# Two more pairs turned by DMA, turns ahead of far loads in the sync queue, and two waits of loads for weight transfers

## The chip, the cores and the metric

The kernel runs on one core of a Trainium2 chip. The core has five engines that run at once, each with its own instruction queue, taken in order: TensorE (PE) for matrix products, VectorE (DVE), ScalarE (ACT) and GpSimd (POOL) for element-wise work, and SyncE (SP), which here only issues transfers. Sixteen DMA engines carry what SP and POOL issue. The metric is the device time in microseconds, the median of three runs.

## The reference

`q`, `k` and `v` have the shape (4, 8, 768, 64): batch, heads, positions, width. The first half is attention over blocks of 64 keys; each query keeps its own block and the three with the highest gate score. The second half is a Fourier mixing, a normalisation and an MLP.

```python
k_rep = k.reshape(B, H, n_blocks, block, D).mean(axis=3)
gate_scores = np.einsum('bhsd,bhnd->bhsn', q, k_rep)
...
top_idx = np.argsort(gate_scores, axis=-1)[..., -top_k:]
...
scores = scale * np.matmul(q, k.transpose(0, 1, 3, 2))
mask = mask & (pos[:, None] >= pos[None, :])
...
return np.matmul(attn, v).astype(np.float32)
```
```python
X = np.fft.fft(x, axis=1)
X = np.fft.fft(X, axis=2)
u = x + np.real(X).astype(np.float32)
...
un = (u - mu) / np.sqrt(var + 1e-06)
ch = np.maximum(un @ w_ch1, 0.0) @ w_ch2
return (u + ch).astype(np.float32)
```

`x` is the attention output of one batch, 768 × 512; `w_ch1` is 512 × 2048 and `w_ch2` 2048 × 512. Inputs and output are float32.

## The kernel before

**Pairs.** `attention(p)` treats two heads at a time, 16 pairs in all, four to a batch. For a pair it loads `k`, `q` and `v` of both heads (six transfers, `load`, issued at line 476 on SP's queue), casts them to float16 (`_copy`, lines 833 and 834) and forms the residuals of `q` and `k` (lines 589 and 594, on POOL for most pairs). `k` and `q` must then be turned, so that the width lies on partitions. Up to pair 6 this is done on PE: `k_turn` (line 606) makes six 128 × 128 transposes for both heads together, `q_turn` (line 672) six for each head, into a PSUM bank, and DVE or ACT copies the bank out (two copies for `k`, two for `q`, lines 833 and 834). From pair 7 on (`TURN_K = 7` for `k`, a literal 7 for `q`) it is done by DMA transposes on SP's queue: two of `k` (line 614) and two of `q` (line 663). Then come the key sums (line 635), their spread (line 652), the gates (line 692, or 687 from pair 6 on), the choice of the top three (lines 706 to 744; from pair 6 on POOL sets the own block at line 739), the turn of the mask (line 751), its writing under the turned `q` (line 761), the scores (line 784) with the exponential on ACT (line 796) and, from pair 5 on, the causal select on POOL (line 802), and the product with `v` (line 814), which DVE normalises into `x` (lines 823 and 826).

**Batches.** `fourier(b)` follows the four pairs of a batch: sums on DVE (lines 846 to 867), products on PE (885 to 929), `u` (lines 944 to 967), statistics and the normalised rows (lines 974 to 1005), and their turn into `unT`, by SP's DMA transposes (line 1017) except for the first three row tiles of batch 0, which PE turns (line 1025). `mlp(b)` is the up-projection (line 1129), the ReLU (1141 on ACT, 1143 on DVE), the down-projection (1158), the addition (1164) and the output. The last batch's down-projection goes by seven block products (1103).

**Weights.** `w1` comes in eight transfers and `w2` in eight more, cast on the way, issued by POOL (line 480). Each has a planned release: 37.0 + 1.8 i for `w1`, `W2` + 1.8 g for `w2`, with `W2 = 55.0`.

**Order.** All operations are given to a planner, `Plan`, with a rank, the engines that may run them with a cost, and what they read and write. `schedule` lays them out on the five queues by start time and then rank. `search` repeats this with random shifts of ranks and releases, grouped by rank or by release, and keeps a shift that doesn't lengthen the plan. The program's instructions are emitted in the order of the plan found; after that each engine's queue is fixed, and on the chip an instruction waits only for its semaphores. Where the plan leaves PE idle before 75 us, `filler` (line 498) puts in products whose result nobody reads. For pair 7 (`p == HP + 3`) the loads name `("w1", 3, 1)`, the last transfer of `w1`, as read; that orders the plan but is no wait on the chip. The loads of pairs 6 and later use two of three slots in turn (`slot`), so pair 8 takes the slot of pair 6, and pair 7 that of pair 4.

Of the kernel before, what the change touches and what calls it, by code (L numbers as in the profile page):

```python
# [81 lines left out]

class Op:
    __slots__ = ("i", "rank", "engs", "fn", "deps", "users", "ps", "wait", "ready",
                 "done", "eng", "start", "dma", "port", "rel", "fill", "hold", "turn")


class Plan:
# [21 lines left out]
        return p  # L110

    def op(self, rank, engs, fn, r=(), w=(), ps=(), dma=0.0, port=False, pre=(), after=(), rel=0.0,
           turn=False):
        o = Op()
        o.turn = turn
        o.rel, o.fill, o.hold = rel, 0, None
        o.i, o.rank, o.engs, o.fn = len(self.ops), rank, engs, fn
        o.deps, o.users, o.ps, o.dma, o.port = set(), [], list(ps), dma, port
        o.eng = o.start = o.done = None
        for k in r:  # L120
            if k in self.last_w:
# [12 lines left out]
        for k in w:  # L134
            self.last_w[k] = o.i
            self.readers[k] = []
        for p in o.ps:
            if p in self.last_w and p not in r and p not in w:
                o.deps.add(self.last_w[p])
            p.left += 1  # L140
        o.deps.discard(o.i)
        self.ops.append(o)
        return o
# [12 lines left out]
    def search(self, rounds, seed):  # L156
# [1 line left out]
        rng = random.Random(seed)  # L158
        groups = {}
        for o in self.ops:  # L160
            if 0 < o.rank < 30000:
                groups.setdefault(("rank", o.rank), []).append(o)
            if o.rel > 59.0:
                groups.setdefault(("rel", o.rel), []).append(o)
# [3 lines left out]
        for _ in range(rounds):  # L168
            what = rng.random()
# [158 lines left out]

LATE = 2600
SYM = (1, 2, 3)  # L330
W2 = 55.0
TURN_K = 7


def release(p):
# [24 lines left out]
def kernel(  # L360
# [12 lines left out]
    HP = H // 2  # L373
# [7 lines left out]
    eng = dict(PE=nc.tensor, ACT=nc.scalar, DVE=nc.vector, POOL=nc.gpsimd, SP=nc.sync)  # L381
# [13 lines left out]
    w1 = sb([128, 4, DF], F16, "w1")  # L395
    w2 = sb([128, NIT, DM], F16, "w2")
# [75 lines left out]
    P = Plan()  # L472


    def dma(rank, e, dst, src, w, us, r=(), issue=0.58, rel=0.0):
        P.op(rank, {e: issue if e != "POOL" else 0.65}, lambda x, n: eng[x].dma_start(dst, src),  # L476
             r=r, w=w, dma=us, rel=rel)

    def weight(rel, dst, src, w):
        P.op(-1000, {"POOL": 0.65}, lambda x, n: nc.gpsimd.dma_start(out=dst, in_=src),  # L480
# [46 lines left out]
    def slot(p):  # L527
        return p % 3 if p < 6 else p % 2

    def load(p, rank, what, e, q_="SP", r=()):  # L530
# [30 lines left out]
    def attention(p):  # L561
# [8 lines left out]
        if p:  # L570
            at_ = 1.7 + 0.1 * p if p < 3 else base - 2900
            for e in range(2):
                load(p, at_, "k", e, r=[("w1", 3, 1)] if p == HP + 3 else ())
                load(p, at_, "q", e, r=[("w1", 3, 1)] if p == HP + 3 else ())
            for e in range(2):
                load(p, at_ + (0.1 if p < 3 else 500), "v", e,
                     r=[("w1", 3, 1)] if p == HP + 3 else ())
        for e in range(2):
            hi = qhl[h2][:, e, :, AT[e]:AT[e] + 64]
            lo = qhl[h2][:, e, 1:NST, 64 - AT[e]:128 - AT[e]]  # L580
# [29 lines left out]
                 w=[tk], ps=[tk], pre=[("ki", 0, g3), ("ki", 1, g3)])  # L610
        for e in range(2):
            if p >= TURN_K:
                P.op(base + 16, {"SP": 1.4},
                     lambda x, n, e=e: nc.sync.dma_start_transpose(
                         out=ki_all[:, g3, 3 * e:3 * e + 3].rearrange("p s e c -> p (s e) c"),
                         in_=kx[h2][:, 3 * e:3 * e + 3, :].rearrange("p s c -> p (s c)")),
                     r=[("k16", h2, 0), ("k16", h2, 1), ("kone", h2)], w=[("ki", e, g3)],
                     pre=[("ki", 1 - e, g3)], turn=True)
                continue
# [38 lines left out]
                                 .rearrange("p (e c) -> p e c", e=2)),  # L658
              r=[ks], w=[("gh", g2)], ps=[ks])
        for e in range(2):  # L660
            if p >= 7:
                P.op(base + 14 + e, {"SP": 1.4},
                     lambda x, n, e=e: nc.sync.dma_start_transpose(
                         out=QG[e][g3].rearrange("p (s c) -> p s c", s=NST),
                         in_=qhl[h2][:, e].rearrange("p s c -> p (s c)")),
# [568 lines left out]
```

## Time and profile before

| | |
|---|---|
| median of 3 runs | 292.82 us (292.0 to 293.37) |
| profiled execution, device time | 294.43 us |
| its span, first to last instruction | 292.7 us |
| PE, DVE, ACT, POOL busy | 285.5, 216.0, 185.5, 142.0 us |
| matrix products on PE | 2965 |
| read from HBM, written | 28.58 MB, 6.29 MB |
| granted TensorE clock | 1.000 |

In the lines of the profile a group shows its source line, engine and operation, its output and inputs by the program's names, and after the bar the busy time and the mean in ns. A window shows the busy time of each engine in a stretch of the span. In a timeline the first number is the start in us and the second the length; brackets give idle time before, and what ended it. `SPq` is SP's queue, where a transfer's issue is counted, and "to landing" is from issue to completion. A matmul's record contains its pipeline's fill, so the steps of the chain of waits, rather than the means of groups, tell how much PE time a run of matmuls takes.

### The profile page before, as it was taken

How to read it: one execution, taken by the hardware profiler on the slowest of the kernel's cores; microseconds unless marked ns; L12 is line 12 of the kernel's file. 1: busy time of each engine (PE TensorE's matmuls, PEld its weight loads, DVE VectorE, ACT ScalarE, POOL GpSimd, SP SyncE). 2: the span in 40 equal slices, each digit the busy share in tenths (PEclk: the TensorE clock that was granted, in tenths of full speed). 3: DMA queues.
4: the chain of work that ended last, by engine and by line, in shares of the span. 5: the costliest groups of instructions: out<-in, count | busy, mean ns of one | idle time of the engine just before them, and what ended most of it. 6: DMA issues, size and time to landing. Idle time of an engine off the chain costs nothing.

```text
span 292.7 us, 8027 instructions
## 1 busy us (share of the span) xinstructions
PE 285.5 (98%) x2965; PEld 191.9 (66%) x2965; DVE 216.0 (74%) x744; ACT 185.5 (63%) x419; POOL 142.0 (49%) x269
## 2 busy tenths in 40 slices
PE   8999999999999999999899999999999999999995
PEld 3778777776656686566556676556655754566884
DVE  5879898899634879986255869989818796057884
ACT  3469999787925587479617866939672681577000
POOL 7467987667776638787608473870220030000000
PEclk9999999999999999999999999999999999999999
DMA  8999998999889977878869549454001006300132
GB/s 209 266 236 231 232 211 133 207 236 217 133 180 212 211 179 158 198 168 192 154 112 226 147 91 188 88 136 105 3 35 45 31 0 115 102 2 0 36 111 72
DMA packets 123191, 41.04 MB, mean 140 GB/s; under 512 B 115608, under 2 KB 119352, under 8 KB 123152
## 3 DMA queue, kind: packets, MB, share of 16 engines
q1 hardware_dynamic: 118672, 35.67, 55.4%
q0 software_dynamic: 3552, 4.56, 9.3%
q8 instruction: 23, 0.38, 0.5%
q10 hardware_dynamic: 928, 0.30, 0.4%
q14 instruction: 16, 0.13, 0.2%
HBM read 28.58 MB, written 6.29 MB: 119 GB/s over the span
## 4 chain that ended last, share of the span: by engine, by line
PE 86%; DMA 5%; SPq 3%; ACT 1%; POOL 1%; issue 1%; DVE 1%; ACTq 0%
PE bank L1129 25%; PE bank L1158 21%; PE bank L784 11%; PE bank L1103 6%; PE bank L814 6%; PE bank L498 5%; DMA loads<-in_q_dram 4%; SPq L476 3%; PE bank L885 2%; PE bank L635 1%; DMA turned<-turned 1%; PE bank L672 1%; PE bank L779 1%; PE bank L692 1%; PE bank L606 1%; PE bank L751 1%
## 5 line engine op out<-in xcount | busy, mean ns | idle before, releaser
L796 ACT ACTIVATE turned<-bank 128x512 f16<-128x512 f32 x192 | 89.5, 576 | 24.0 <-PE bank L784 23.8
L1129 PE MATMUL bank<-unT,w 128*128 128x384 f16 x512 | 90.5, 326 | 0.2 <-DVE u L967 0.2
L1141 ACT ACTIVATE hT<-bank 128x384 f16<-128x384 f32 x117 | 57.4, 498 | 29.7 <-PE bank L1129 27.0
L1158 PE MATMUL bank<-w,hT 128*128 128x512 f16 x288 | 67.9, 379 | 0.0
L1129 PEld LDWEIGHTS <-w 128*128 128x128 f16 x512 | 47.7, 97 | 29.4 <-issue 0.5
L784 PE MATMUL bank<-turned,keys 128*128 128x128 f16 (+6 forms) x384 | 50.2, 259 | 0.2 <-DVE u L967 0.2
L1158 PEld LDWEIGHTS <-hT 128*128 128x128 f16 x288 | 26.7, 97 | 27.8
L802 POOL TENSOR_SCALAR_AFFINE_SELECT turned<-turned 128x512 f16<-128x512 f16 (+1 forms) x44 | 22.7, 538 | 30.6 <-ACT turned L796 15.3
L784 PEld LDWEIGHTS <-keys 128*128 128x128 f16 (+1 forms) x384 | 29.3, 97 | 12.0 <-issue 0.4
L814 PEld LDWEIGHTS <-turned 128*128 128x128 f16 x672 | 24.2, 97 | 5.3 <-ACT turned L796 1.1
L594 POOL TENSOR_TENSOR loads<-loads 128x384 f16<-128x384 f32 x25 | 23.0, 919 | 6.3 <-DVE fs L867 2.4
L814 PE MATMUL bank<-small,turned 128*128 128x65 f16 x672 | 25.6, 193 | 0.2 <-ACT turned L796 0.2
L761 DVE TENSOR_SCALAR turned<-bank 12x384 f16<-12x384 f16 x64 | 20.4, 318 | 5.7 <-PE bank L751 3.2
L589 POOL TENSOR_TENSOR turned<-loads,turned 128x320 f16<-128x320 f32 x26 | 20.8, 800 | 5.4 <-DVE turned L834 3.0
L498 PE MATMUL bank<-bsb 128*128 128x512 f16 x75 | 21.9, 422 | 1.3 <-DVE bsb L487 1.3
L1164 DVE TENSOR_TENSOR u<-bank,u 128x512 f32<-128x512 f32 x18 | 12.4, 686 | 11.8 <-PE bank L1158 11.7
L955 POOL TENSOR_TENSOR u<-u,bsb 128x255 f32<-128x255 f32 x10 | 7.3, 726 | 22.7 <-DVE u L959 18.4
L826 DVE TENSOR_TENSOR x<-bank,small 128x384 f16<-128x384 f32 x32 | 17.7, 553 | 0.7
L823 DVE RECIPROCAL small<-bank 128x6 f32<-128x6 f32 x32 | 6.1, 191 | 13.7 <-PE bank L814 13.3
L974 DVE BATCH_NORM_STATS2 small<-u 128x6 f32<-128x512 f32 x24 | 16.0, 678 | 0.1
L834 POOL CAST small<-loads 128x384 f16<-128x384 f32 x24 | 11.8, 507 | 8.4 <-DVE pm L857 3.3
L1109 DVE TENSOR_TENSOR u<-u,bank 128x256 f32<-128x256 f32 x36 | 13.1, 415 | 3.2 <-PE bank L1103 2.2
(138 smaller groups left out, 438.7 us busy)
## 6 DMA issues: line engine op xcount, KB each, us to landing
loads<-in_k_dram SPq DMA_DIRECT2D x28, 192.0 KB, 3.4
loads<-in_v_dram SPq DMA_DIRECT2D x28, 192.0 KB, 3.7
loads<-in_q_dram SPq DMA_DIRECT2D x26, 192.0 KB, 3.5
out_dram<-u SPq DMA_DIRECT2D x18, 256.0 KB, 2.4
w<-in_moe_w_ch_dram POOLq DMA_DIRECT2D x16, 256.0 KB, 6.8
out_dram<-u SPq DMA_DIRECT2D x12, 128.0 KB, 1.7
hT<-in_k_dram SPq DMA_DIRECT2D x4, 192.0 KB, 3.8
hT<-in_q_dram SPq DMA_DIRECT2D x4, 192.0 KB, 3.9
```

The source lines that it names most:

```text
L498: nc.tensor.matmul(bank32[P.SPARE], warm[:, 0:128], warm, start=True, stop=True)
L589: lambda x, n, hi=hi, lo=lo, e=e: eng[x].tensor_tensor(out=lo, in0=qn[a][:, e, 1:NST], in1=hi[:, 1:NST], op=OP.subtract),
L594: lambda x, n, kh=kh, kl=kl, e=e: eng[x].tensor_tensor(out=kl, in0=kn[a][:, :, e, :], in1=kh, op=OP.subtract),
L761: nc.vector.tensor_scalar(out=rows[:, i::2, :], in0=turned[at:at + NB, 0:3 - i, :], scalar1=-NEG, scalar2=NEG, op0=OP.mult, op1=OP.add)
L784: nc.tensor.matmul(bank32[sp.bank][:, co:co + a1 - a0], KI[e][g3][0:ROWS[e], jt, :], QG[e][g3][0:ROWS[e], a0:a1], start=not added, stop=no ...
L796: lambda x, n, sp=sp, pt=pt, at=at, wid=wid: nc.scalar.activation(out=pt[:, at:at + wid], in_=bank32[sp.bank][:, 0:wid], func=AF.Exp, scal ...
L802: lambda x, n, pt=pt, at=at, nd=nd: nc.gpsimd.affine_select(out=pt[:, at:at + 128 * nd].rearrange("p (a c) -> p a c", a=nd), in_=pt[:, at: ...
L814: nc.tensor.matmul(o[:, st, 0:65], pt[:, col:col + 128], V16[v4][:, e, jt, 0:65], start=(i == 0), stop=(i == 20))
L826: lambda x, n, rc=rc, o_=o_, h=h: nc.vector.tensor_tensor(out=xb[b % 3][:, :, 64 * h:64 * h + 64], in0=o_()[:, :, 0:64], in1=rc.to_broadca ...
L1129: nc.tensor.matmul(bank32[hp_.bank][:, 0:384], w1[:, dt, 128 * it:128 * it + 128], unT[:, dt, 384 * hf:384 * hf + 384], start=(dt == 0), s ...
L1141: nc.scalar.activation(out=o, in_=i_, func=AF.Relu)
L1158: nc.tensor.matmul(bank32[cp.bank], hT[hf][:, it, 128 * j:128 * j + 128], w2[:, it, :], start=(it == 0), stop=(it == NIT - 1))
```

## The change

`TURN_K` becomes 5 and a new `TURN_Q = 5` takes the place of the literal 7, so `k` and `q` of pairs 5 and 6 are turned by DMA as well. The ranks of all DMA turns of `q` and `k` go down by `TOP = 2000`, two pairs' worth, against other work of the same queue, loads among it. The planner's `op` takes `behind`, a list of keys whose last writers come first; these become real dependencies of the instruction. By it the loads of pair 7 wait for the transfer `("w1", 2, 1)`, the seventh of the weights, and those of pair 8 for `("w2", 6)`, the fifteenth; pair 7's former plan-only order behind `("w1", 3, 1)` goes. `W2` is 56.0 instead of 55.0. The search has 800 rounds instead of 700 and another seed, and may now also shift groups with ranks between -5000 and 0.

```diff
-           turn=False):
+           turn=False, behind=()):
         o = Op()
+        o.behind = [self.last_w[k] for k in behind]
...
+        o.deps.update(o.behind)
         o.deps.discard(o.i)
...
-            if 0 < o.rank < 30000:
+            if -5000 < o.rank < 30000:
...
-W2 = 55.0
-TURN_K = 7
+W2 = 56.0
+BEHIND = {7: [("w1", 2, 1)], 8: [("w2", 6)]}
+TOP = 2000
+TURN_Q = 5
+TURN_K = 5
...
-            [(t, i, e)], 0.72 if p < 1 else 0.88, r=r,
+            [(t, i, e)], 0.72 if p < 1 else 0.88, behind=BEHIND.get(p, ()),
...
-                load(p, at_, "k", e, r=[("w1", 3, 1)] if p == HP + 3 else ())
-                load(p, at_, "q", e, r=[("w1", 3, 1)] if p == HP + 3 else ())
+                load(p, at_, "k", e)
+                load(p, at_, "q", e)
...
-                P.op(base + 16, {"SP": 1.4},
+                P.op(base - TOP + 16, {"SP": 1.4},
...
-            if p >= 7:
-                P.op(base + 14 + e, {"SP": 1.4},
+            if p >= TURN_Q:
+                P.op(base - TOP + 14 + e, {"SP": 1.4},
...
-        for o in P.search(700, 10):
+        for o in P.search(800, 12):
             filler(o.fill)
             made[o.i] = o.fn(o.eng, o)
-            if o.hold is not None:
-                tc.add_manual_dep(made[o.i].ins, made[o.hold.i].ins.name, mybir.DependencyInfo(
-                    mybir.DependencyClass.Sync, mybir.DependencyReason.DATA), reason="port")
+            for i in ([o.hold.i] if o.hold is not None else []) + o.behind:
+                tc.add_manual_dep(made[o.i].ins, made[i].ins.name, mybir.DependencyInfo(
+                    mybir.DependencyClass.Sync, mybir.DependencyReason.DATA), reason="order")
```

More of the change, by code (lines that the diff above doesn't have):

```diff
@@ L84 @@
     __slots__ = ("i", "rank", "engs", "fn", "deps", "users", "ps", "wait", "ready",
-                 "done", "eng", "start", "dma", "port", "rel", "fill", "hold", "turn")
+                 "done", "eng", "start", "dma", "port", "rel", "fill", "hold", "turn", "behind")
 class Plan:
@@ L472, with dma @@
     P = Plan()
-    def dma(rank, e, dst, src, w, us, r=(), issue=0.58, rel=0.0):
+    def dma(rank, e, dst, src, w, us, r=(), issue=0.58, rel=0.0, behind=()):
         P.op(rank, {e: issue if e != "POOL" else 0.65}, lambda x, n: eng[x].dma_start(dst, src),
-             r=r, w=w, dma=us, rel=rel)
+             r=r, w=w, dma=us, rel=rel, behind=behind)
     def weight(rel, dst, src, w):
@@ L528, in slot, with load @@
         return p % 3 if p < 6 else p % 2
-    def load(p, rank, what, e, q_="SP", r=()):
+    def load(p, rank, what, e, q_="SP"):
         b, hp = divmod(p, HP)
@@ L572, in attention @@
             for e in range(2):
-                load(p, at_, "k", e, r=[("w1", 3, 1)] if p == HP + 3 else ())
-                load(p, at_, "q", e, r=[("w1", 3, 1)] if p == HP + 3 else ())
+                load(p, at_, "k", e)
+                load(p, at_, "q", e)
             for e in range(2):
-                load(p, at_ + (0.1 if p < 3 else 500), "v", e,
-                     r=[("w1", 3, 1)] if p == HP + 3 else ())
+                load(p, at_ + (0.1 if p < 3 else 500), "v", e)
         for e in range(2):
```

## The prediction, made before the changed kernel ran

> **What bounds the kernel now.** I read the page's first parts, then the busy time by stage, then the waits of PE after the first up-projection.
>
> ```profile
> span 292.7 us, 8027 instructions
> PE 285.5 (98%) x2965; PEld 191.9 (66%) x2965; DVE 216.0 (74%) x744; ACT 185.5 (63%) x419; POOL 142.0 (49%) x269
> ...
> PEclk9999999999999999999999999999999999999999
> ```
> ```profile
> core 0: us, PE busy (x) PEld busy (x) DVE busy (x) ACT busy (x) POOL busy (x), PEclk, DMA share, GB/s
> ...
> 53.00:67.47 14.47, 14.28 (x169) 11.02 (x169) 13.69 (x46) 11.47 (x25) 9.69 (x18) 1.00 1.19 223
> ...
> 80.00:140.00 60.00, 59.71 (x634) 38.71 (x633) 43.94 (x154) 39.53 (x94) 42.70 (x87) 1.00 0.85 184
> 140.00:150.00 10.00, 8.81 (x83) 5.31 (x80) 3.43 (x20) 4.71 (x10) 4.07 (x10) 1.00 0.79 164
> 150.00:240.00 90.00, 90.00 (x866) 57.84 (x864) 69.67 (x212) 60.09 (x141) 37.50 (x75) 1.00 0.41 91
> 240.00:289.30 49.30, 49.23 (x343) 33.37 (x341) 31.60 (x92) 18.06 (x37) 0.67 (x1) 1.00 0.23 60
> ```
> ```profile
> PE bank L687 <- DMA turned<-turned: 1.2, 1, 1.2
> ```
> ```profile
> 53.00:67.50 14.50, 4.88 (x19) 1.66 (x18) 1.00 1.19 223
> 67.50:80.00 12.50, 0.00 (x0) 0.00 (x0) 1.00 1.07 176
> ```
>
> The clock is full in every slice (PEclk). A window's columns are its length, then busy time and count by engine. From 80 us to 289.3 us PE works without a break, but for one gap of 1.2 us near 146. Before 67.5 us its 98% is padded: the last windows are of the fillers (L498) alone, 4.88 us of the 14.5 us before MLP 0. In that stretch DVE is the full engine (13.69 of 14.47 us): it does the Fourier step of batch 0, which the first up-projection needs. So the time is the start of that up-projection, plus PE's work behind it, plus the gaps in that work. Work that leaves PE before 67.5 us helps only if DVE lets the up-projection start sooner.
>
> **The transfers of the same stretch** are the second thing to see.
>
> ```profile
> 46.10 0.37 SPq L476 DMA_DIRECT2D loads<-in_k_dram  x1
> ```
> ```profile
> 64.35 11.78 DMA loads<-in_q_dram
> ```
> ```profile
> 49.25 1.10 POOL L480 DMA_DIRECT2D w<-in_moe_w_ch_dram  x2
> ...
> 67.61 1.43 POOL L480 DMA_DIRECT2D w<-in_moe_w_ch_dram  x2
> ...
> 72.94 0.51 POOL L834 CAST loads<-loads 128x384 f16<-128x384 f32 x1 [1.47 <-DMA loads<-in_k_dram]
> ...
> 76.18 0.53 POOL L834 CAST turned<-loads 128x384 f16<-128x384 f32 x1 [1.79 <-DMA loads<-in_q_dram]
> ```
> The second fence is the chain of waits, the third POOL's timeline. Counted by pair, SP issues the loads of pair 8 first (from 46.10) and those of pair 7 last; its q takes 11.78 us beside the weights, and POOL idles for it.
>
> **The change, part by part.** *Turns of pairs 5 and 6.* 36 transposes leave PE.
>
> ```profile
> 50.05 0.34 PE bank L672 x6
> ...
> 50.68 0.89 PE bank L498 x4
> ```
> Six cost 0.34 us (those of k have the same shape), so PE loses 6 × 0.34 = 2.04 us. The changed program's order has 78 fillers where 75 stood, which adds 3 × 0.22 = 0.66. All else on PE is the same: net −1.4 us. Almost all of that (−1.5, the rest moved behind) lies ahead of the first up-projection. Can DVE follow? Eight evictions go away as well; the rows for 30 to 67 us are
>
> ```profile
> L726 DVE MAX8 mx<-gsb 128x8 f32<-128x12 f32 x40 | 3.2, 155 | 0.0
> L834 DVE COPY turned<-bank 128x768 f16<-128x768 f16 x6 | 3.1, 548 | 0.0
> ...
> L967 DVE TENSOR_TENSOR u<-bank,x 128x512 f32<-128x512 f32 x4 | 2.5, 677 | 0.0
> ...
> L730 DVE TENSOR_TENSOR gmp<-gsb,mx 128x120 f16<-128x120 f32 x1 | 0.3, 271 | 0.0
> L710 DVE TENSOR_TENSOR gsb<-bank,gsb 128x120 f32<-128x120 f32 x1 | 0.3, 264 | 0.0
> ```
> Between the last x of pair 3 and the normalising pass L1005, DVE's new order lacks two q copies (1.1), pair 6's ten MAX8 (40 take 3.2: 0.8), its L710 and L730 (0.5) and a small copy (0.2), and has one L967 more (0.68): 2.6 − 0.7 = 1.9 us less. So DVE can give the 1.4 us, and I take −1.4 in full. Bounds: 0 if DVE's chain is held by something else, −1.9.
>
> *What the turns cost elsewhere.* Eight DMA transposes join SP's queue.
>
> ```profile
> L663 SPq DMA_TRANSPOSE turned<-turned x18: 1209/1238/1512, 77.5 to 201.3; - x18
> ...
> DMA to landing us min/median/max: 2.5/2.6/4.5
> ```
> ```profile
> 47.63 0.78 POOL L589 TENSOR_TENSOR turned<-loads,turned 128x320 f16<-128x320 f32 x1 [1.07 <-DVE kg L834]
> ```
> ```profile
> 59.64 0.40 PE L687 MATMUL bank<-kg,turned 128*128 128x24 f16 x10
> ...
> 67.24 0.33 PE L751 MATMUL bank<-small,gmp 128*128 128x128 f16 x3
> 67.47 1.46 PE L1129 MATMUL bank<-unT,w 128*128 128x384 f16 x8
> ```
> Each holds SP 1.24 us, 10 us in all, at a place where SP waited anyway (its loads of 46 to 67 us move behind). Late is at worst the second q turn of pair 6: its input is ready at 47.63 + 0.78 = 48.4; one k turn goes ahead (1.24), so it lands at 49.7 + 2.6 = 52.3. No turn of the trace ran beside the weights; the nearest rows are the loads that did:
>
> ```profile
> w<-in_moe_w_ch_dram POOLq DMA_DIRECT2D x3, 256.0 KB, 7.6
> loads<-in_k_dram SPq DMA_DIRECT2D x2, 192.0 KB, 8.3
> loads<-in_q_dram SPq DMA_DIRECT2D x2, 192.0 KB, 8.7
> ```
> ```profile
> loads<-in_q_dram SPq DMA_DIRECT2D x26, 192.0 KB, 3.5
> ```
> The first three were issued from 46 to 51 us. The fourth is the page's, over all q loads of SP: 3.5 us, so company costs up to 8.7 − 3.5 = 5.2 us and the turn lands at 57.5. The gates that need it stood at 59.64; what stands ahead of them in PE's new order, each instruction at its row's time, is 2.4 us more: 62.0. Covered, with 4.5 us to spare.
>
> A rule that speaks against this part: the Trainium skill (VectorE: DVE Perf Modes, The three transpose paths, and its Rules for kernel authors) would turn a 128×128 tile on TensorE, at 390 ns there against 1309 ns by DMA. By its figure six tiles take an estimated 7.9 us; by the row above they land in 2.6, so the trace does not bear that figure out. It is priced among the rivals.
>
> *The waits.* Pair 7's loads wait for the seventh weight transfer, pair 8's for the fifteenth. Behind them in SP's queue stand pair 7's turns, then the loads of pairs 8 and 9 and pair 8's turns, then the first output and batch 0's last three unT turns. The seventh transfer left as second of the two at 49.25, at 49.8; at 7.6 us it landed near 57.5. With pair 8's six loads gone from that time it should do as those of 38 to 46 us did:
>
> ```profile
> w<-in_moe_w_ch_dram POOLq DMA_DIRECT2D x5, 256.0 KB, 5.4
> ```
> That is near 55.2, so the four k and q loads leave from 55 to 58 and land, at 3.5 to 8.7 us, by 61.5 to 66.7. I take 64, the middle: few weights are in flight then, since w2 waits on POOL for the select of pair 5 and an `fs` sum. Who waits: four casts on POOL, and behind them in its new order the last weight issue (0.7) and the four memsets of pair 6's mask (1.07, below). The mask is turned at L751, 67.24 before, and by the same count 1.2 later now: 68.4.
>
> ```profile
> 65.57 1.07 POOL L739 MEMSET gmp<- 64x5 f16 x4
> ```
> 64 + 0.5 + 0.7 + 1.1 = 66.3: in time by 2 us. At the slow end, 66.7, it is 0.6 late. Pair 8's loads come up in SP's queue only after pair 7's turns, near 71, when the fifteenth transfer is down or nearly so (it left at 67.61, the first of the last two, and six loads fewer compete); they land by 77, while POOL still has pair 7's residuals and the select of pair 6 ahead of their casts. I cost this wait at nothing; where that cover is gone pair 8's sums on PE are late, one for one.
>
> *Turns ahead of far loads, W2 one later, a longer search.* These reorder, at no work.
>
> ```profile
> 137.32 4.13 SPq L1017 DMA_TRANSPOSE unT<-x  x3
> 141.51 1.17 SPq L476 DMA_DIRECT2D loads<-in_v_dram  x2
> 142.77 1.21 SPq L663 DMA_TRANSPOSE turned<-turned  x1
> ```
> The gap at 146 is the turn issued at 142.77, queued behind two far v loads and three unT turns. The new order puts attention 5 to 10 us earlier against the MLP there, so this gap (1.2 us) goes; but a new order of 225 us on a full PE may open its own. Bounds: −1.2 to +2.4 (two such gaps more than are lost); I take −0.6, half the gap.
>
> **Sum.** −1.4 − 0.6 = −2.0 us: the span 292.7 becomes 290.7. The profiled execution itself took 294.43 (1.7 around its span), and the runs shown have a median of 292.82, close to the span; so 290.8 us.
>
> **Rivals.** (1) *Hidden anyway.* The up-projection still starts at 67.5 and the freed PE time turns into fillers; what moved behind (0.1) and half the gap at 146 leave 292.82 + 0.1 − 0.6 = 292.3. For it: PE has 4.88 us of fillers there already. Against: DVE, the full engine, loses 1.9 us.
>
> (2) *More.* The start gains DVE's full 1.9, the gap at 146 goes whole and nothing opens: 292.82 − 1.9 − 1.2 = 289.7. Against: a new order rarely has no gap of its own.
>
> (3) *Pair 7's loads hold POOL: slower.* The seventh weight lands at 57.5 as before, the loads leave until 60.5 and take 8.7 to 11.78 us: 69.2 to 72.3. Cast, issue and memsets bring pair 6's mask to 71.5 to 74.6 against 68.4. PE stands in order at L751, with the up-projection behind it: 3.1 to 6.2 us, the middle 4.6. 292.82 − 1.4 + 4.6 = 296.0. It decides from the point where the fourth load lands after 66.1. For it: every load of 46 to 65 us was this slow. Against: six of them are what the wait moves away.
>
> (4) *Late turns: slower.* Beside the weights the turns could take 8.7 us, as the loads did, and one after the other: pair 6's last two then end at 48.4 + 17.4 = 65.8, 3.8 behind the gates: 292.82 − 1.4 + 3.8 = 295.2. By the skill's estimated 7.9 us each they would end at 64.2, and the time be 293.6. Against: the 18 turns of L663 landed in 2.5 to 4.5 us while SP issued one every 1.24.
>
> (5) *The change doesn't do what it says:* SP reaches the loads only after the awaited weights. For pair 8 that is my forecast; it has no time of its own.
>
> **How the numbers follow.** Forecast 0.48, (1) 0.17, (2) 0.17, (3) 0.13, (4) 0.05. The forecast's own range is 289.9 to 291.8. Half a per cent, about what the measurement can tell from no change, is 1.46 us: faster is under 291.36, slower over 294.28. Faster: three quarters of the forecast and (2), with a tenth of (1): 0.36 + 0.17 + 0.02 = 0.55. Slower: nearly all of (3) and (4), 0.17. Same: the rest, 0.28. The range 289.0 to 295.5 takes in (1), (2) and the lower part of (3).
>
> **What would show it.** First up-projection near 66 us, not 67.5; 78 fillers, and 60 and 30 transposes where L672 and L606 have 84 and 42; pair 6's gates and mask without idle PE in front of them; pair 7's fourth load down before 66 us; no DMA-ended gap at PE after 80 us longer than 1 us. Pair 7's casts waiting on POOL past 66 us, or a turn landing later than 62, would make it wrong.

## The result and the profile after

The changed kernel takes 315.84 us (median of 4 runs, 314.53 to 318.65) where the kernel before took 293.1 us (4 runs, 292.0 to 293.6) on the same chip: a ratio of 1.0794, with a 95% interval of 1.0715 to 1.0874. The forecast was 290.8 us and its range ended at 295.5, so the forecast is wrong in its sign. The profiled execution is one of the four, 315.75 us with a span of 314.0. Here and below, a ratio leaves out runs that took over 1.5% longer than the fastest run of the same kernel.

The page of the changed kernel, its span and a few of its slices (one slice is 7.85 us):

```profile
span 314.0 us, 7964 instructions
...
PE   8999992696939999999999999999999999999995
...
PEclk9999999599859999999999999999999999999999
...
GB/s 212 249 255 225 263 135 98 73 116 164 196 179 248 161 152 223 201 200 168 139 203 130 228 178 180 28 77 145 84 4 0 69 84 84 69 0 0 19 118 69
```

PE has holes in the seventh and eighth, the tenth and the twelfth slice, around 55, 78 and 88 us, and within each of them the granted clock falls to a half, for some us beyond its end; the rest is as full as before. In the first and largest, of all places, the transfers move least of the first 100 us: 98 and 73 GB/s. The same by windows, the last three being the stretches at half the clock:

```profile
core 0: us, PE busy (x) PEld busy (x) DVE busy (x) ACT busy (x) POOL busy (x), PEclk, DMA share, GB/s
...
50.00:60.00 10.00, 2.33 (x43) 2.12 (x44) 1.20 (x12) 0.73 (x3) 0.49 (x2) 0.68 1.38 76
60.00:70.00 10.00, 9.42 (x97) 6.54 (x95) 5.95 (x16) 5.72 (x13) 4.07 (x7) 0.80 1.20 106
...
100.00:314.00 214.00, 210.11 (x1940) 136.88 (x1935) 154.99 (x489) 121.77 (x285) 82.87 (x167) 1.00 0.52 113
```
```profile
53.70:63.94 10.24, 5.86 (x49) 3.85 (x50) 2.49 (x16) 2.55 (x7) 1.30 (x2) 0.50 1.31 80
77.59:81.00 3.41, 2.94 (x12) 1.17 (x13) 1.38 (x4) 0.00 (x0) 0.40 (x1) 0.50 1.22 196
87.83:94.66 6.83, 3.59 (x18) 2.24 (x19) 2.83 (x8) 0.98 (x3) 5.94 (x12) 0.50 0.91 162
```

From 50 to 60 us every engine is nearly idle, while the DMA engines count as busy (share 1.38) and move 76 GB/s; before, the stretch of 53 to 67 us moved 223. What PE waited for, by the view of waits (total, times, longest), and where, by PE's timeline:

```profile
PE bank L696 <- DMA turned<-turned: 9.2, 2, 6.7
PE bank L755 <- POOL gmp L743: 5.3, 1, 5.3
PE bank L691 <- DMA turned<-turned: 2.5, 1, 2.5
```
```profile
50.94 0.41 PE L696 MATMUL bank<-kg,turned 128*128 128x12 f16 x10 [2.50 <-DMA turned<-turned]
58.08 0.44 PE L696 MATMUL bank<-kg,turned 128*128 128x12 f16 x10 [6.72 <-DMA turned<-turned]
...
78.06 0.31 PE L691 MATMUL bank<-kg,turned 128*128 128x24 f16 x5 [2.51 <-DMA turned<-turned]
...
83.02 2.76 PE L1133 MATMUL bank<-unT,w 128*128 128x384 f16 x16
91.07 0.50 PE L755 MATMUL bank<-small,gmp 128*128 128x128 f16 x3 [5.29 <-POOL gmp L743]
```

In front of both halves of pair 5's gates, the second half of pair 6's gates and pair 6's mask, PE stands idle for 2.5 + 6.7 + 2.5 + 5.3 = 17.0 us, and the first up-projection starts at 83.02 us instead of 67.47. The turns themselves, from issue to landing, of 38 to 80 us:

```profile
L667 SPq DMA_TRANSPOSE turned<-turned x4: 1373/2026/3847, 40.0 to 69.8; - x4
...
DMA to landing us min/median/max: 8.2/11.0/14.7
```
```profile
L618 SPq DMA_TRANSPOSE keys<-loads x4: 1237/3541/7669, 44.9 to 66.1; - x4
...
DMA to landing us min/median/max: 9.2/15.8/19.8
```

The q turns of the trace before landed in 2.5 to 4.5 us, those of k in 2.5 to 4.9. Here none of the eight is faster than 8.2, and one issue holds SP for 7.7 us instead of 1.24. The 14 weight transfers beside them take a median of 9.1 us. How the lateness is handed on shows in DVE's, POOL's and SP's rows of the timeline:

```profile
58.62 0.28 DVE L719 TENSOR_TENSOR gsb<-bank,small 128x120 f32<-128x120 f32 x1 [9.62 <-PE bank L696]
...
61.22 0.79 POOL L593 TENSOR_TENSOR turned<-loads,turned 128x320 f16<-128x320 f32 x1 [10.72 <-DVE fs L871]
...
73.78 0.53 SPq L481 DMA_DIRECT2D loads<-in_k_dram  x1
...
89.25 0.51 POOL L838 CAST turned<-loads 128x384 f16<-128x384 f32 x1 [0.20 <-DMA loads<-in_q_dram]
89.70 0.72 POOL L485 DMA_DIRECT2D w<-in_moe_w_ch_dram  x1
90.42 0.60 POOL L743 MEMSET gmp<- 64x5 f16 x4
```

DVE works in order: it stands 9.62 us at pair 5's gate evictions, with Fourier's `fs` behind them. POOL stands 10.72 us for that `fs`, with pair 6's q residuals behind it, so pair 6's second q turn, which the prediction had ready at 48.4, leaves at 69.84. SP gets to pair 7's loads at 73.78; they fly beside seven weight transfers, their last q lands at 89.2, and their casts keep POOL from pair 6's mask until 90.42.

As an account of PE's time the sum agrees with the span: 17.0 us of waits, about 6.2 us of clock (half of the 12.4 us that PE worked at 0.50, an estimate from the three windows), less the two microseconds or so that left PE's work and the gap at 146, makes 21; the span is 21.3 longer.

### The profile page after: what moved, and what is told of

Its sections match the earlier page's. It is cut to its first block, busy times and chain, and to the rows that moved or that the text cites. A ratio compares the mean times of both kernels' runs of the same rounds, so it can differ in the third digit from the quotient of the medians.

```text
span 314.0 us, 7964 instructions
## 1 busy us (share of the span) xinstructions
PE 290.8 (93%) x2932; PEld 192.3 (61%) x2932; DVE 218.8 (70%) x753; ACT 178.6 (57%) x408; POOL 137.4 (44%) x263
## 4 chain that ended last, share of the span: by engine, by line
PE 78%; DMA 8%; ACT 6%; DVE 2%; SPq 2%; POOL 1%; issue 1%; ACTq 0%
PE bank L1133 26%; PE bank L1162 20%; PE bank L788 9%; PE bank L1107 6%; PE bank L818 5%; DMA turned<-turned 5%; ACT turned L800 4%; PE bank L503 4%; DMA loads<-in_q_dram 4%; PE bank L889 2%; PE bank L639 1%; SPq L481 1%; ACT small L837 1%; PE bank L755 1%; SPq L667 1%
## 5 line engine op out<-in xcount | busy, mean ns | idle before, releaser
L1145 ACT ACTIVATE hT<-bank 128x384 f16<-128x384 f32 x109 | 53.7, 496 | 43.3 <-PE bank L1133 42.0
L1162 PE MATMUL bank<-w,hT 128*128 128x512 f16 x288 | 69.2, 379 | 0.0
L1133 PEld LDWEIGHTS <-w 128*128 128x128 f16 x512 | 48.9, 98 | 31.2 <-issue 1.2
L788 PE MATMUL bank<-turned,keys 76*128 76x128 f16 (+7 forms) x384 | 51.3, 263 | 0.0
L788 PEld LDWEIGHTS <-keys 76*128 76x128 f16 (+1 forms) x384 | 30.2, 99 | 13.5 <-issue 1.1
L806 POOL TENSOR_SCALAR_AFFINE_SELECT turned<-turned 128x512 f16<-128x512 f16 (+1 forms) x44 | 23.6, 555 | 33.5 <-ACT turned L800 24.2
L503 PE MATMUL bank<-bsb 128*128 128x512 f16 x78 | 24.0, 447 | 1.3 <-DVE bsb L492 1.3
L838 POOL CAST loads<-loads 128x384 f16<-128x384 f32 x24 | 12.1, 504 | 13.3 <-issue 7.2
L837 ACT CAST small<-bank 128x386 f16<-128x386 f32 (+1 forms) x21 | 9.3, 482 | 14.5 <-PE bank L889 6.8
L838 POOL CAST small<-loads 128x384 f16<-128x384 f32 x22 | 11.0, 509 | 9.1 <-PE bank L818 2.2
```

The lines of the kernel that those rows point to most:

```text
L503: nc.tensor.matmul(bank32[P.SPARE], warm[:, 0:128], warm, start=True, stop=True)
L788: nc.tensor.matmul(bank32[sp.bank][:, co:co + a1 - a0], KI[e][g3][0:ROWS[e], jt, :], QG[e][g3][0:ROWS[e], a0:a1], start=not added, stop=no ...
L806: lambda x, n, pt=pt, at=at, nd=nd: nc.gpsimd.affine_select(out=pt[:, at:at + 128 * nd].rearrange("p (a c) -> p a c", a=nd), in_=pt[:, at: ...
L838: return eng[x].tensor_copy(out=dst, in_=src)
L1133: nc.tensor.matmul(bank32[hp_.bank][:, 0:384], w1[:, dt, 128 * it:128 * it + 128], unT[:, dt, 384 * hf:384 * hf + 384], start=(dt == 0), s ...
L1145: nc.scalar.activation(out=o, in_=i_, func=AF.Relu)
```

## The experiments

The question was what makes a turn take 8 to 20 us: the company of the weights (theory A), the place in the order, or the waits. Times are medians; the kernel before ran beside each group, at 292.82 us (first four), 293.3 (next four) and 293.43 (last four).

**Turns back on PE.** Everything of the change but the turns.

```
-TURN_Q = 5
-TURN_K = 5
+TURN_Q = 7
+TURN_K = 7
```

> The changed kernel with TURN_Q and TURN_K at 7 again: pairs 5 and 6 are turned by PE, all else of the change stays (waits of the loads, ranks, W2, search). Theory A (a DMA turn beside the weight transfers takes 8 to 20 us, and everything behind it in order waits): the 21 us are gone, 290 to 295 us, no PE wait over 2 us between 40 and 95 us. Theory B (the waits of the loads and the new order cost the time): it stays over 308 us. Theory C (both): 300 to 306 us.

Measured: 297.28 us (ratio 1.0149, 1.0106 to 1.0191), span 294.2, clock 1.0. So 18.6 of the 22.7 us hang on the turns of two pairs. The other 4.5 us over the kernel before are more than theory A allowed for, and less than B or C.

**Only the turns.** The kernel before, with q and k of pairs 5 and 6 turned by transfers; ranks, waits and search as before, so the order is planned anew.

```
-TURN_K = 7
+TURN_K = 5
...
-            if p >= 7:
+            if p >= TURN_K:
```

> The kernel before with the turns of pairs 5 and 6 by DMA and nothing else of the change (search 700 with its seed, no waits, old ranks). Theory A: turns land 8 to 20 us after their issue and the time is over 305 us. Theory B: turns land within 5 us and the time stays within 2 us of the kernel before.

Measured: 299.50 us (1.0234, 1.0199 to 1.0269), span 297.3, first up-projection at 70.64. The waits of PE and the transfers of 38 to 62 us (KB each, median to landing):

```profile
PE bank L692 <- DMA turned<-turned: 3.0, 1, 3.0
...
PE bank L687 <- DMA turned<-turned: 1.2, 3, 0.5
```
```profile
w<-in_moe_w_ch_dram POOLq DMA_DIRECT2D x9, 256.0 KB, 6.7
loads<-in_v_dram SPq DMA_DIRECT2D x2, 192.0 KB, 4.3
turned<-turned SPq DMA_TRANSPOSE x4, 7.3
keys<-loads SPq DMA_TRANSPOSE x4, 7.0
```

The sign is that of theory A, the size is not: the eight turns landed in 3.9 to 11.9 us and cost 3.0 us of waits at pair 5's gates (the waits of L687 belong to later pairs, from 89 us on), and the time rose by 6.7 us in all. How late a turn gets differs with the order; that of after has the later ones.

**No weights in flight.** The 16 weight transfers become memsets on POOL, so the product with the weights is left out; order and turns are those of after. It was run twice, first with a single execution.

```
-        P.op(-1000, {"POOL": 0.65}, lambda x, n: nc.gpsimd.dma_start(out=dst, in_=src),
+        P.op(-1000, {"POOL": 0.65}, lambda x, n: nc.gpsimd.memset(dst, 0.01),
```

> The changed kernel with its 16 weight transfers left out: POOL writes a constant into the weight tiles instead, so the MLP's result isn't the reference's. Theory A: the eight turns of pairs 5 and 6 land 2.5 to 5 us after issue, PE waits for no turn over 1.5 us before 95 us, and the time is 288 to 294 us. Theory B: the gates of pairs 5 and 6 still wait, over 305 us. Theory D (the turns are slow by themselves at that place, for instance beside the far loads): turns over 8 us though no weight moves.

> Once more the changed kernel with its weight transfers replaced by memsets on POOL (so the output lacks the weights), now timed: its one profile had its first gates 2 us later than after's with the same order, at a clock of 0.5 from 8.7 to 12.1 us. Theory R: without that start 291 to 294 us, turns of 2.5 to 4.5 us. Rival (the order itself is 2 us worse): 294.5 to 297 us with a start like that of after.

Measured: 295.28 us in the single execution, whose first gates came 2 us later (12.47 against 10.54 us); then 293.46 us (10 runs, 1.0004 of before, 0.9973 to 1.0036), span 291.6. The q turns of 38 to 80 us in the second kernel, two of pair 7 among them:

```profile
L667 SPq DMA_TRANSPOSE turned<-turned x6: 1210/1223/1992, 40.0 to 72.8; - x6
...
DMA to landing us min/median/max: 2.5/2.9/4.4
```

The same turns, in the same place of the same order, land in 2.9 us, and no matmul waits for one. Company it is. But even with that cured the time is that of the kernel before, 1.0004; how far the memsets themselves cost time here is looked at below, under PE's transposes.

**Turns beside chosen company.** A kernel by itself, no part of the reference: four turns on SP beside four weight pieces or eight loads, in stages.

```
+STAGES = [("none", 4), ("w1 cast", 0), ("w1 cast", 4), ("w2 cast", 0), ("w2 cast", 4),
+          ("w1 plain", 0), ("w1 plain", 4), ("w1 plain act", 0), ("w1 plain act", 4),
+          ("loads act", 0), ("loads act", 4), ("none", 4), ("w1 cast", 4)]
```

> A kernel of its own that only measures transfers and writes zeros as output: in 13 stages, one after the other, four DMA turns of 128x768 float16 run alone, or beside four 128x1024 weight pieces cast by the transfer in rows of w1 or of w2, the same pieces of w1 without a cast from POOL or from ACT, or eight loads of 192 KB in packets of 256 B. Theory A1 (any company from HBM): a turn takes over 8 us beside all of them. Theory A2 (the cast transfers of w1, with their 2 KB packets): over 8 us beside w1 with cast, 2.5 to 5 us beside w2, plain pieces and loads. Theory A3 (any transfer issued by POOL): slow beside cast and plain pieces of POOL, not beside those of ACT. Theory D: no company slows a turn beyond 5 us.

Measured, issue to landing of the four turns: alone; beside cast pieces from POOL; beside the same pieces plain from ACT; beside eight 192-KB loads.

```profile
DMA to landing us min/median/max: 2.8/2.8/2.8
...
DMA to landing us min/median/max: 4.8/8.1/10.9
...
DMA to landing us min/median/max: 4.8/11.4/13.8
...
DMA to landing us min/median/max: 2.9/5.3/6.3
```

None of the theories holds as written. Neither the cast nor POOL's queue makes the difference: a plain piece from ACT is no better company. Loads, of as many bytes each as the turn and in rows of 256 B, delay it least, though there are somewhat fewer bytes of them: 8 × 192 KB against the 4 × 512 KB that the pieces read.

**The length of the rows.** Two runs: the pieces of that kernel cut into runs of 1024, 512, 256 and 128 elements, and after itself with all weights in runs of 128 elements and the same order on PE, DVE, ACT and SP.

```
-    w1 = sb([128, 4, DF], F16, "w1")
+    w1 = sb([128, 16, 4, 128], F16, "w1")
...
-                weight(37.0 + 1.8 * i, w1[:, dt, 1024 * hf:1024 * hf + 1024],
+                weight(37.0 + 1.8 * i, w1[:, 8 * hf:8 * hf + 8, dt, :],
...
-                weight(W2 + 1.8 * g, w2[:, 2 * g:2 * g + 2, :],
+                weight(W2 + 1.8 * g, w2[:, 8 * h:8 * h + 8, 128 * n:128 * n + 128],
```

> A kernel by itself, no part of the reference: four turns of 128x768 on SP beside four cast weight pieces of 512 KB on POOL, the pieces cut into runs of 1024, 512, 256 and 128 elements (4096 to 512 B read, 2048 to 256 B written), each also without turns, and runs of 1024 once more at the end. Theory A1 (length of the row): the slowest turn falls from 10 to 11 us with runs of 1024 to under 7 us with runs of 128, about in steps. Theory A2 (bytes): 9 to 12 us at each length. Either way the pieces alone take 4.5 to 8 us at each length, unless short rows cost the transfer itself.

> The changed kernel in the same order on PE, DVE, ACT and SP, with the 16 weight transfers of the same bytes cut so that one run of consecutive elements is 128 (256 B written) instead of 1024 or 512. Theory A1 (a turn's short packets wait behind the weights' long ones, so that the length of a row decides): the eight turns of pairs 5 and 6 land within 3 to 8 us instead of 8 to 20, PE waits under 3 us for them, and the time is 292 to 298 us. Theory A2 (the bytes decide, whatever the rows): turns of 8 to 20 us and 313 to 318 us as after. Theory A3 (short rows make the weights themselves so slow that the up-projection waits for them): turns under 8 us, but weight transfers over 12 us and a time over 300 us.

Measured by itself: median landing of four turns alone, then beside runs of 1024, 512, 256 and 128 elements.

```profile
dst<-src SPq DMA_TRANSPOSE x4, 2.8
...
dst<-src SPq DMA_TRANSPOSE x4, 7.9
...
dst<-src SPq DMA_TRANSPOSE x4, 10.6
...
dst<-src SPq DMA_TRANSPOSE x4, 9.1
...
dst<-src SPq DMA_TRANSPOSE x4, 8.0
```

In the kernel: 310.53 us (6 runs, 1.0552, 1.0505 to 1.06), turns of 3.5 to 12.2 us, weight transfers of 5.5 to 17.9. The row length is not the cause: its theory A1 falls in both. The time is some 5 us shorter than after's, without a cure; since POOL's order and the order in which w2 arrives are other ones too, even these 5 us are not shown to be the rows'.

**The waits of the loads.** After, in its own order, without the added waits.

```
-            for i in ([o.hold.i] if o.hold is not None else []) + o.behind:
+            for i in ([o.hold.i] if o.hold is not None else []):
```

> The changed kernel in its own order on every engine, without the added waits of the loads of pairs 7 and 8 for weight transfers. Theory A (those waits never wait: SP comes to pair 7's loads at 73.8 us, when the seventh weight transfer has been down since 66.1, and to pair 8's at 94.8, when the fifteenth has been down since 87.7): the same time as after, 314.5 to 317 us, and the loads leave within 0.5 us of where they left. Theory B (the waits hold SP and what stands behind it): 3 us faster or more, under 313 us.

Measured: 317.39 us (4 runs, 315.57 to 319.61). The loads left at 71.87 and 93.79 us instead of 73.78 and 94.84, that is as SP came to them. In after's order the waits cost nothing: the seventh weight had landed at 66.10 and the fifteenth at 87.67, before SP came to the loads. The loads moved by more than the half microsecond of theory A, since the turns ahead of them landed at other times in this execution.

**PE kept busy.** Fillers in the idle stretches, against the loss of clock.

```
+                filler({5: (10, 30), 6: (0, 11)}.get(p, (0, 0))[e])
...
+            filler(23 if p == 6 else 0)
```

> The changed kernel with 74 more fillers (writes to the spare bank, nothing of the result): 10 and 30 ahead of the two halves of pair 5's gates, 11 ahead of the second half of pair 6's gates, 23 ahead of pair 6's mask turn, that is a little less than PE stood idle there (2.5, 6.7, 2.5 and 5.3 us, at 0.22 us each). Theory A (the idle stretches cost twice: PE waits, and then works at half of its granted clock, 21.0 us at 0.5 in the profile of after): the 0.5 stretches go, the clock is 1.0 throughout and the time falls by about half of the busy time in them, 4 to 7 us, to 309 to 312 us. Theory B (the clock is a symptom that costs nothing, since PE waits for others anyway): 314.5 to 317 us whatever the clock.

Measured: 319.33 us (4 runs, 315.95 to 321.91), so nothing is gained. In the profiled execution (the longest of the four) the turns were later still, PE used up its fillers, stood 12.1 us at the first half of pair 5's gates and had the half clock again, from 52.5 us on for 13.7; it doesn't test the theory. The other three left no trace, but their mean clock was 0.983 to 0.994, where after's runs had 0.962 to 0.967, and the best of them took 315.95 us at 0.994. That speaks for theory B, a clock that cost little, unless the turns were later in these runs too. The 6.2 us above stay an estimate. The transfers of the profiled execution from 48 to 52.5 us, however, show the stall at its plainest:

```profile
GB/s 61 25 39 20 0 20 2 18 20 0 20 20 0 23 0 20 20 0 20 2 18 20 0 20 20 0 23 0 20 20 0 20 2 18 20 0 20 20 0 11
DMA packets 75, 0.07 MB, mean 15 GB/s; under 512 B 48, under 2 KB 48, under 8 KB 75
```

Two turns, three weight transfers and a load are in flight, a third turn joins them, and 15 GB/s move. By the packet records 19 packets that started from 46.72 to 48.24 all end from 52.75 to 52.82; in between a single stream of packets moves, 172 ns for one of 2048 B and 31 ns for one of 256 B in turn. It looks like a rendezvous (all have to meet before any goes on): the turn's packets stand on each engine until the last engine has come to that turn.

In after's own trace such groups stand too (a 256-B packet alone takes 18 ns, a 2048-B one 172):

```
packets started us   ended us         packets   longest us
46.11 to 47.09       47.68 to 47.76       9        1.6
51.53 to 52.17       52.94 to 53.06      18        1.5
72.28 to 72.52       73.80 to 73.84      18        1.5
```

**A rendezvous, tested.** A kernel by itself: transfers from ACT that touch eight partitions load part of the 16 DMA engines (the busy share then is a half, so about eight of them); then two turns, or two ordinary loads of the same bytes; then two weight pieces.

```
+            for i, n, r in company[kind]:
+                rows(i, n, r)
+            for i in range(2):
+                if what == "turn":
+                    turn(i)
+                if what == "load":
+                    nc.sync.dma_start(out=ld[i], in_=(q if i else k)[0, i].rearrange("(st p) d -> p st d", p=128))
+            for i in range(2):
+                nc.gpsimd.dma_start(out=w16[i], in_=w1_part(i))
```

> A kernel by itself, no part of the reference: four transfers from ACT that touch one partition (24 KB each) or eight partitions (192 KB each) load few of the 16 DMA engines; then two turns, or two ordinary loads of 192 KB, on SP; then two weight pieces on POOL. Theory R (rendezvous: a turn's packets stand on every DMA engine until the last engine has come to that turn, and what is queued behind them stands too): beside uneven transfers the first turn takes as long as the fullest engine, its packets on the free engines are recorded with more than 0.3 us (18 to 31 ns alone) and end within 0.15 us of one another; the ordinary loads show no such group. Theory S (share of capacity only): no groups of long packets, and the turn is delayed no more than the ordinary load. If the uneven transfers turn out to be spread over all engines by the hardware, neither is tested.

The transfers of one partition, 48 packets of 2 KB in all, were down within about 3 us, so they test nothing. Those of eight partitions do. What the weight pieces behind them took (KB each, median us): without turn or load, with the two turns, with the two loads.

```profile
half<-in_moe_w_ch_dram POOLq DMA_DIRECT2D x2, 256.0 KB, 13.7
...
half<-in_moe_w_ch_dram POOLq DMA_DIRECT2D x2, 256.0 KB, 19.4
...
half<-in_moe_w_ch_dram POOLq DMA_DIRECT2D x2, 256.0 KB, 14.6
```

The packet records of the two stages, counted:

```
two turns  (first issued at 126.06): 256-B packets ended from 127 to 128: 249; from 128 to 137: none;
           nine that started from 127.75 to 127.88 ended from 139.48 to 139.54; longest 11.78 us
           2048-B packets of the loaded engines, 128 to 137: 25 to 28 ended in each us (24 to 28 without turns)
two loads  (first issued at 152.50): 256-B packets longest 0.32 us; no such group
```

The turn came to the free engines at once, stood there for 11.7 us until the loaded ones were done, and the weights behind it stood with it: 5.7 us more than without. The load of the same bytes did neither (0.9 us). Where no transfer of eight partitions ran, the pieces behind two turns took 5.8 us: it is the unevenness that makes a turn a hindrance. Theory R holds, and capacity alone (S) falls.

**Weights after the turns.** After, its first eight weight transfers due 10 us later.

```
-                weight(37.0 + 1.8 * i, w1[:, dt, 1024 * hf:1024 * hf + 1024],
+                weight(47.0 + 1.8 * i, w1[:, dt, 1024 * hf:1024 * hf + 1024],
```

> The changed kernel with its first eight weight transfers due 10 us later in the plan (47.0 instead of 37.0), which puts them behind pair 6's last two q residuals in POOL's order, so that hardly any weights are in flight beside the eight turns of pairs 5 and 6; the rest of the order is planned anew. Theory R (it is the weights' company that made the turns late): the eight turns land within 2.5 to 6 us, PE waits under 1.5 us for turns in all, the clock stays at 1.0, and the time is 291 to 296 us. Rival (the turns in that place are late whatever flies beside them, or the weights now come too late for the up-projection): PE waits of 4 us or more, 298 us or more.

Measured: 298.39 us (three runs, 297.57 to 299.37; 1.017, 1.0096 to 1.0244), span 295.9, clock 1.0. A fourth run took 311.27 us at a mean clock of 0.972; it left no trace, but a clock like that came with long idle stretches of PE in after. PE's waits for a turn in the profiled execution:

```profile
PE bank L691 <- DMA turned<-turned: 0.4, 1, 0.4
```

The three turns issued by 45 us, before the first weight (47.1), landed in 3.4 to 4.0 us, the next four, beside weights, in 6.9 to 10.4, the last in 3.9. So the company decides once more, turn by turn, but theory R's "2.5 to 6 us" holds for four of the eight only: the weights were not out of the way. It is right about PE's waits and, in three of four runs, about the clock; the first up-projection is back at 67.22. The time missed its range by 2.4 us and lies in the rival's. The new plan has gaps of its own, 1.7, 1.3 and 1.0 us at 129 to 134 us, and the chain that ended last runs through one of the late turns (issued at 50.52, 9.0 us).

**Turns on PE, once more.** Like the first run, with the search kept from moving the first pair's loads, which there put v ahead of k.

```
-            if -5000 < o.rank < 30000:
+            if 0 < o.rank < 30000 or o.rank == -1000:
```

> The changed kernel with q and k of pairs 5 and 6 turned on PE as before, like the run that put the turns back, but with the search kept from moving the loads of the first pair (there it had put v ahead of k, and the first gates came 2 us later). Theory (the rest of the change is worth about nothing, the 2 us of that run came from its start): 291.5 to 294.5 us, first up-projection at 66.5 to 68.5. Rival (the waits or the turns put ahead cost time by themselves): 296 us or more again.

Measured: 298.13 us (1.0165, 1.0094 to 1.0237), span 295.1, first up-projection at 68.90. The start was not it, and the time is the one that the rival named. Three plans drawn anew by the longer search (the first run, this one and the one above) take 4.5 to 5.0 us more than the kernel before, while after's own plan without weights takes the same. Part of that may be the plan by itself, but it is not shown. In the first run SP did stand for a weight ahead of pair 7's loads, for 19.2 us, yet the chain that ended last has no transfer of a load in it from 36 us on, so there, as far as the chain tells, the wait cost nothing. Here SP stood for 18.5 and 4.4 us, and the chain runs through pair 8's last q load, which left at 80.12, behind pair 7's turns; PE also waits 1.5 us for an `unT` turn. What the waits and the new order of SP's queue cost where turns are on time stays open.

## Why the prediction was wrong

**What bounds the kernel** was read rightly: nothing behind 100 us changed (PE works 210.1 of 214 us there), and the time is that of the first up-projection.

**The step that failed** is the landing of the turns, whose cost the sum put at nothing: "the nearest rows are the loads that did: ... 3.5 us, so company costs up to 8.7 − 3.5 = 5.2 us and the turn lands at 57.5", "Covered, with 4.5 us to spare". The sum took a turn for a transfer with as many bytes as a load. It is one in bytes and alone (2.8 us), but the test of the rendezvous shows that it has to come together on the DMA engines: there it stood 11.7 us for the loaded ones, and the weights behind it were 5.7 us late. Beside weights it took 8.2 to 19.8 us in the kernel, where loads beside weights had taken 8.3 to 11.8; PE's waits that follow from it are the 17.0 us above. Pair 5's two q turns, which the sum never priced on their own since pair 6's were "at worst", landed at 50.90 and 58.03; PE stood 2.5 and then 6.7 us for them.

**What was late next** failed with it. The prediction took pair 6's input as ready at 48.4 and let it wait only in SP's queue. In fact pair 6's q residuals stand behind DVE (9.62 us) and POOL (10.72 us), both of which work in order and waited for pair 5's gates. The second q turn of pair 6 landed at 78.01, not 52.3 to 57.5; its gates came at 78.06 instead of 62.0.

**Rival (4), late turns**, had the cause and one chance in twenty. Its price, 8.7 us each and 3.8 us in all, used the same row of loads. What was said against it, that 18 turns landed in 2.5 to 4.5 us, was no evidence: no weight was in flight beside those (77.5 to 201.3 us; the last weight landed at 76.72). **Rival (3)**, pair 7's loads holding POOL, happened as well, by 5.3 us against its 4.6, but as a consequence: the loads left at 73.78, after the turns, not at 60.5.

**The waits of the loads cost nothing**: right for after's order, and shown there by taking them away. For pair 7 the reason was another: rival (5)'s mechanism held for it too, SP came after the weight had landed. The prediction's own working of pair 7's wait comes out where PE turns pairs 5 and 6: the seventh weight landed at 57.02 and 55.22 us in these two runs (55.2 forecast), and the fourth load was down at 64.70 and 60.52 (64 forecast).

**Minus 1.4 us from PE's transposes**: not settled. The fillers and transposes are as counted (78, 60 and 30). In after the turns hide it; after's order without weights starts its up-projection at 67.68 instead of 67.47. The rows of that stretch for before and for after without weights:

```profile
30.00:67.47 37.47, 36.76 (x580) 28.99 (x578) 34.56 (x131) 33.40 (x75) 28.72 (x49) 1.00 1.05 204
```
```profile
30.00:67.68 37.68, 36.28 (x523) 26.71 (x522) 33.31 (x122) 29.14 (x67) 30.19 (x43) 1.00 0.69 147
```

and DVE's rows in it, first one of before, then those of after without weights, with a wait of PE:

```profile
L1005 DVE TENSOR_SCALAR x<-u,small 128x512 f16<-128x512 f32 x2 | 1.1, 613 | 0.0
```
```profile
L1009 DVE TENSOR_SCALAR x<-u,small 128x512 f16<-128x512 f32 x2 | 2.5, 1314 | 0.0
...
L838 DVE CAST tr<-bank 128x384 f16<-128x384 f32 x3 | 1.7, 592 | 1.6 <-ACT small L837 1.6
...
L719 DVE TENSOR_TENSOR gsb<-bank,small 128x120 f32<-128x120 f32 x3 | 0.8, 283 | 1.1 <-PE bank L696 1.1
```
```profile
PE bank L1029 <- DVE x L1009: 0.7, 1, 0.7
```

DVE did lose work (34.56 to 33.31 us, 1.25 of the 1.9 counted), and stood idle for as much more: 37.47 − 34.56 = 2.9 us before, 37.68 − 33.31 = 4.4 now, mostly for ACT and for pair gates. That speaks for the bound "0 if DVE's chain is held by something else". But the test has a cost of its own right in front of the up-projection: while POOL wrote the constants that stand for the weights (63.09 to 65.83 us), the two normalising passes took 2.5 us from 64.01 on, where they take 1.1 before and 0.99 in after, and PE stood 0.7 us for them. Without that the start would be near 66.9 (an estimate: 67.68 less the 0.74 that PE stood). So of the 1.4 us between nothing and about half a microsecond is seen, and rival (1), hidden anyway, is near what the change would have been, without being shown.

**Minus 0.6 for the gap at 146**: right as far as it shows, and small. The gap is gone in after (no wait for a turn behind 78 us), and after's order without weights needs 291.6 − 67.68 = 223.9 us behind its first up-projection, against 225.2 in a profiled execution of before that was itself 1.6 us above the median. The bound for other plans, up to 2.4 us of new gaps, may be too small: three newly drawn plans took 4.5 to 5.0 us more.

**The Trainium skill's rule** (VectorE: DVE Perf Modes, The three transpose paths) that was set aside would have kept the tiles on TensorE. Its price is still not what the runs show: six tiles alone land in 2.8 us, not an estimated 7.9. What speaks for the rule here is the company, which that table does not count. The Trainium skill's sentence that "A transpose next to ordinary DMAs needs nothing" (DMA: Bandwidth & Descriptors, Rules for kernel authors) stands in a row on correctness; taken as one on time it is not borne out here: 2.8 us alone, 4.8 to 13.8 next to weight pieces.

## What to carry to other kernels

Price a DMA transpose by the traffic that flies beside it, and look at the DMA share of that stretch first (1.19 here): where transfers are backed up unevenly, it waits for the fullest engine and holds up everyone else's transfers. Put turns where nothing heavy is in flight, or leave them on an engine; and before moving work off an engine, ask whether its successors' inputs come any sooner. Where a planner draws the whole order anew for every test, the order is part of what is measured (three such tests took 4.5 to 5.0 us more here, and why is open); test one part of a change in the plan of the whole where that can be done, and look what the test itself slows down.

## What the hardware showed that was not expected

A DMA transpose acts as a rendezvous of the DMA engines: beside about eight loaded engines its packets stood 11.7 us on the free ones and ended within 0.06 us of one another, with the weights behind them 5.7 us late, where an ordinary load of the same 192 KB left no such group. A busy DMA share can thus be standing time: 1.38 of share at 76 GB/s, and in one stretch of 4.2 us (48.2 to 52.4, with the fillers) a single stream of packets moved. Packets of 256 B to 2 KB that were recorded with over 0.6 us, from 36 to 100 us, summed over engines:

```
kernel (profiled execution)          packets   sum us    its time us
before                                  33       39       294.43
after, no weights in flight             40       37       293.46
turns on PE, start kept                 68       80       296.89
weights after turns                     76       75       297.57
only the turns                          79       84       298.99
turns back on PE                        94       95       295.92
after, fillers                         136      248       321.91
after, weights in short rows           145      168       310.59
after, loads not held                  175      303       315.84
after                                  206      213       315.75
```

The sum goes with the time only roughly, since standing packets cost nothing where no engine waits for them: with the turns back on PE most of them come from 76 to 92 us, beside `unT`'s and later pairs' turns. What made the engines uneven in the kernel in the first place was not found; two executions of the same order on every engine, after and after with its loads not held, differ in it (213 and 303 us) and still took the same time.
